# Softmax maxima taken from one group's projected queries, and four output projections in one step

## The chip, the cores and the metric

The kernel runs on one core of a Trainium2 chip. The metric is the device time of one execution in microseconds (us). A core has a matrix engine (TensorE, PE in the tables; its weight loads are PEld), a vector engine (VectorE, DVE), a scalar engine (ScalarE, ACT), a general engine (GpSimd, POOL) and a queue engine (SyncE, SP), which in this kernel issues every DMA. Each works through its own list of instructions in order and waits on semaphores where it needs a result of another.

## What is computed

Two layers, each made of attention and a feed-forward block, over 2048 positions of 448 numbers. The same weights serve both layers.

```python
def _A_ref(x, wq, wk, wv, wo):                    # x: 1 x 2048 x 448, 16 heads of 28
    q = (x @ wq).reshape(B, S, H, Dh)             # 16 heads of queries
    k = x @ wk                                    # one head of keys for all
    v = x @ wv                                    # one head of values for all
    scores = einsum(q, k) * Dh ** -0.5
    p = softmax(scores)
    return (p @ v, heads joined) @ wo
def _B_ref(x, w_gate, w_up, w_down):
    return (silu(x @ w_gate) * (x @ w_up)) @ w_down
x = x + _A_ref(layernorm(x)); x = x + _B_ref(layernorm(x))    # and both once more
```

## The kernel before, in words

Every matrix product is done with numbers split in two, a rounded high part and the rest, and two or three products are added up. The 2048 positions are cut in four chunks of 512 (`c`); the 16 heads are four groups of four (`g`). A unit of attention is one group of one chunk: 16 units, in the order of the list `GR`.

**Projection stage** (`project`, `q`, `finish`). The columns of `wq`, `wv` and `wk` lie side by side in one weight tile of 512 columns, taken in four blocks of 128 (`m`). Blocks 0 to 2 and the first 64 columns of block 3 are queries, 28 columns of block 3 are values, 28 are keys. For each chunk the blocks are taken in the order `TURN = (3, 0, 1, 2)`, 11 products each (L277). ScalarE copies a block out of PSUM, VectorE or GpSimd makes the low part (L464 to L468), and the pair goes to DRAM as `qd` (L470). After block 3, four DMAs put the keys on four places of `keys` (L476), VectorE turns the values (L478) and four DMAs put them in `vsb` (L480). The tile pair that a block is written to (`halves`) has three buffers, so a copy waits until the DMAs that read the block three before are done. A block of 128 columns holds parts of two groups, so a group's queries come together only when they are read back from DRAM by `stack` (four DMAs, L352) into one of three tiles `qstack`.

**Maxima.** The softmax needs a bound for each query. One product (L368) multiplies a tile `qstack` with a block-diagonal tile of keys (`kdiag`); `rows` (L376 to L386) turns the result on VectorE straight from PSUM, takes the largest of each 32, and one DMA (`qstack<-down`) writes the negated bound into a row of `qstack`. Three of the 16 are done in the projection stage, one of each later 13 in an attention step.

**Attention stage** (`scores`). A unit has 16 steps (`kt`), one for 128 keys: 12 score products (`step`, L541) into a tile of three PSUM banks (two such tiles take turns) and bank 7, two exponentials on ScalarE (L547 for bank 7, L548 for the three), and 4 products with the values two steps later (`pv`, L575). `between_steps` puts other work between a step's scores and the value products, at step 10 of a unit: one maxima product into the free three-bank tile; in units 9 to 12 four transposes for the next feed-forward (`flip`, L248) into the same tile; one output projection of 128 positions (12 products, `outproj`, L527) into bank 7, and its sum on VectorE (L531). A chunk's four output projections fall into four units; those of the third chunk into step 10 and step 13 of units 12 and 13.

**Feed-forward** follows, 14 blocks of the hidden width in pairs. In the first layer its last pair overlaps the first four projections of the second layer (`hand_over`). A last piece of the program, which repeats all in another form if a value ran out of range, is not executed here.

## Time and profile before

| | |
|---|---|
| three runs | 2071.49, 2077.33, 2077.23 us, median 2077.23 |
| profiled execution, its own time | 2076.66 us |
| its span, first to last instruction | 2074.9 us |
| projection of layer 1, from the first `qd` store to the first exponential | 20.0 to 78.5 us |
| attention of layer 1 | 78.5 to 614.2 us |
| feed-forward of layer 1, then projection of layer 2 | 614.2 to 1102.9 us |
| attention of layer 2 | 1102.9 to 1638.6 us |
| feed-forward of layer 2 | 1638.6 to 2074.9 us |

In the tables a row gives the busy time of a group of instructions, the mean length of one, and the time that its engine stood idle just before them, with what ended the idle time behind an arrow. "SPq" is an issue of a DMA on SyncE: the time that the issuing takes, not that of the transfer. In the chain of waits a piece "DMA" is the time from an issue to the landing of its data.

### The profile page before, as it was taken

How to read it: one execution, taken by the hardware profiler on the slowest of the kernel's cores; microseconds unless marked ns; L12 is line 12 of the kernel's file. 1: busy time of each engine (PE TensorE's matmuls, PEld its weight loads, DVE VectorE, ACT ScalarE, POOL GpSimd, SP SyncE). 2: the span in 40 equal slices, each digit the busy share in tenths (PEclk: the TensorE clock that was granted, in tenths of full speed). 3: DMA queues.
4: the chain of work that ended last, by engine and by line, in shares of the span. 5: the costliest groups of instructions: out<-in, count | busy, mean ns of one | idle time of the engine just before them, and what ended most of it. 6: DMA issues, size and time to landing. Idle time of an engine off the chain costs nothing.

```text
span 2074.9 us, 43753 instructions
## 1 busy us (share of the span) xinstructions
PE 2024.9 (98%) x18577; PEld 1303.5 (63%) x18577; DVE 507.9 (24%) x1038; ACT 1301.0 (63%) x2126; POOL 492.2 (24%) x504
## 2 busy tenths in 40 slices
PE   6999999999999999999999999999999999999998
PEld 4533333333348999999874333333333589999997
DVE  6201112112114233222460111121121152333322
ACT  2599988988883333333337998989888643333332
POOL 5202101012202333323341111111122123333321
PEclk9999999999999999999999999999999999999999
DMA  6301101011100111000132110101120001111102
GB/s 187 114 21 41 30 17 30 16 45 31 36 7 23 30 30 30 24 23 25 37 108 78 38 36 19 31 16 30 31 48 19 12 19 30 30 30 30 30 2 74
DMA packets 86590, 78.23 MB, mean 38 GB/s; under 512 B 26736, under 2 KB 66032, under 8 KB 86384
## 3 DMA queue, kind: packets, MB, share of 16 engines
q1 hardware_dynamic: 86384, 75.33, 13.2%
q8 instruction: 148, 2.42, 0.5%
q14 instruction: 58, 0.48, 0.1%
HBM read 51.51 MB, written 18.61 MB: 34 GB/s over the span
## 4 chain that ended last, share of the span: by engine, by line
PE 48%; ACT 44%; DVE 3%; issue 2%; SPq 2%; DMA 1%; POOL 0%; ACTq 0%; DVEq 0%
PE bank L299 38%; ACT pt L548 29%; ACT pt L547 14%; PE bank L527 3%; PE bank L277 3%; PE three L541 1%; PE bank L575 1%; PE bank L248 1%; PE bank L541 1%; SPq L131 1%; PE three L527 1%; DVE xl L258 0%; DVE xn L230 0%; DVE stats L217 0%; PE three L368 0%
## 5 line engine op out<-in xcount | busy, mean ns | idle before, releaser
L548 ACT ACTIVATE pt<-three 128x1536 f32<-128x1536 f32 x512 | 741.7, 1449 | 0.0
L575 PE MATMUL bank<-pt,vsb 128*32 128x512 f32 x4096 | 547.1, 607 | 0.6 <-ACT pt L548 0.6
L541 PEld LDWEIGHTS three<-qstack,keys 32*128 32x128 f32 x4608 | 253.4, 184 | 455.9 <-ACT pt L547 394.4
L541 PE MATMUL three<-qstack,keys 32*128 32x512 f32 x4608 | 503.0, 428 | 7.7 <-ACT q L467 4.4
L541 PE MATMUL bank<-qstack,keys 32*128 32x512 f32 x1536 | 494.7, 427 | 0.5 <-DVE xres L531 0.3
L299 PE MATMUL bank<-xh,wgh 64*128 64x512 f32 x1728 | 470.9, 390 | 0.5
L299 PE MATMUL bank<-xh,wgl 64*128 64x512 f32 x1404 | 382.3, 388 | 0.0
L547 ACT ACTIVATE pt<-bank 128x512 f32<-128x512 f32 x512 | 306.0, 598 | 98.6 <-PE bank L541 96.2
L299 PE MATMUL bank<-xl,wgh 64*128 64x512 f32 x1296 | 350.1, 387 | 0.0
L299 PE MATMUL bank<-wdh,h 64*128 64x448 f32 x1792 | 339.5, 362 | 1.3 <-ACT h L784 0.9
L299 PEld LDWEIGHTS bank<-xh,wgh 64*128 64x128 f32 x1728 | 287.2, 184 | 8.9 <-DVE xl L258 1.6
L299 PEld LDWEIGHTS bank<-wdh,h 64*128 64x128 f32 x1792 | 263.0, 184 | 7.7 <-issue 2.7
L609 POOL TENSOR_TENSOR o<-o 128x512 f32<-128x512 f32 x32 | 41.1, 1284 | 895.3 <-DMA o<-rd 703.3
L541 PEld LDWEIGHTS bank<-qstack,keys 32*128 32x128 f32 x1536 | 244.8, 184 | 4.9 <-DVE xres L531 3.0
L702 POOL TENSOR_TENSOR xres<-stage,xres 128x448 f32<-128x448 f32 x112 | 131.2, 1192 | 488.3 <-ACT stage L701 488.3
L299 PEld LDWEIGHTS bank<-xh,wgl 64*128 64x128 f32 x1404 | 235.3, 184 | 4.1
L306 ACT COPY seen<-bank 128x1 f32<-128x1 f32 x664 | 83.4, 164 | 235.9 <-PE bank L299 234.4
L299 PE MATMUL bank<-wdl,h 64*128 64x448 f32 x896 | 228.0, 364 | 0.0
L299 PEld LDWEIGHTS bank<-xl,wgh 64*128 64x128 f32 x1296 | 215.4, 185 | 2.8
L782 ACT ACTIVATE sg<-bank 128x512 f32<-128x512 f32 x112 | 67.0, 599 | 221.6 <-PE bank L299 212.2
L575 PEld LDWEIGHTS bank<-pt,vsb 128*32 128x32 f32 x4096 | 80.9, 108 | 189.4 <-issue 174.6
L783 DVE TENSOR_TENSOR sg<-bank,sg 128x512 f32<-128x512 f32 x112 | 77.4, 691 | 495.6 <-ACT sg L782 486.6
(115 smaller groups left out, 1731.7 us busy)
## 6 DMA issues: line engine op xcount, KB each, us to landing
qstack<-qd SPq DMA_DIRECT2D x128, 112.0 KB
qd<-q SPq DMA_DIRECT2D x24, 512.0 KB
o<-rd SPq DMA_DIRECT2D x32, 256.0 KB
wdr<-in_B_w_down_dram SPq DMA_DIRECT2D x28, 224.0 KB
wr<-in_B_w_gate_dram SPq DMA_DIRECT2D x28, 192.0 KB
wr<-in_B_w_up_dram SPq DMA_DIRECT2D x28, 192.0 KB
keys<-q SPq DMA_DIRECT2D x32, 112.0 KB
out_dram<-xres SPq DMA_DIRECT2D x16, 224.0 KB
```

The source lines that it names most:

```text
L277: nc.tensor.matmul(po, a, b, start=(i == 0), stop=(i == len(seq) - 1))
L299: nc.tensor.matmul(po, a, b, start=start, stop=stop, skip_group_check=True)
L306: nc.scalar.copy(seen[:, i : i + 1], po[:, 0:1])
L527: nc.tensor.matmul(po[:, 0:D], a[:, g, ts_], b[:, g, :], start=(g + z == 0), stop=(g == NG - 1 and z == 2))
L541: nc.tensor.matmul(three[:, j, :] if j < 3 else one, k[js, ks], q[js, part, :], start=(z == 0), stop=(z == 2), tile_position=(32 * j, 0),)
L547: nc.scalar.activation(pt1, one, AF.Exp, scale=SCALE)
L548: nc.scalar.activation(pt, three, AF.Exp, scale=SCALE)
L575: nc.tensor.matmul(accs[i][32 * j : 32 * j + 32, :], vsb[:, kt, :], pts[n][j], start=(kt == 0), stop=(kt == NT - 1), skip_group_check=True,)
L609: nc.gpsimd.tensor_tensor(rb, oraw, rb, ALU.mult)
L702: nc.gpsimd.tensor_tensor(r, s, r, ALU.add)
L782: nc.scalar.activation(sg, pg[0], AF.Silu)
L783: nc.vector.tensor_tensor(sg, pg[1], sg, ALU.mult)
```

## The change

The weight tile is laid out anew: each of the four blocks now holds the 112 queries of exactly one group, and 16 more columns. Blocks 0 and 1 carry the values in two parts (16 and 12), blocks 2 and 3 the keys in two parts; the order is `TURN = (3, 2, 0, 1)`. So a maxima product takes its moving operand straight from the block's tile, without the way through DRAM, and `kdiag` holds the keys packed in 112 rows.

- All 16 maxima products are made in the projection stage (`maxima`), three blocks after their own. For the first three units `rows` follows as before; for the other 13 the product is copied out of PSUM into a `stage` tile and written to DRAM (`kept`). In attention it is read back into an SBUF tile four steps into a unit, and `rows` works on that, four steps later.
- Each block issues one store of `qd` of 112 rows and then either four DMAs of 12 or 16 rows for `keys` or four for `vsb`; in the first chunk eight more DMAs fill `kdiag` (before: four copies on GpSimd).
- All low parts of the queries are made on VectorE; for chunks 2 and 3 of layer 1 the normalisation moves from VectorE to GpSimd.
- In layer 2 the first three blocks, made while the feed-forward still runs, are read back from DRAM (`fetch`) for their maxima products.
- A chunk's four output projections stand in one step (step 10 of units 4, 8 and 12): three into the banks of the free tile, the fourth into bank 7, and in units 8 and 12 two transposed blocks between them, in bank 7 too.

```diff
-TURN = (3, 0, 1, 2)
+TURN = (3, 2, 0, 1)
...
+            nc.gpsimd.memset(r[:, :, 252:256], 0.0)
+            rows3(r[:, :, 0:224], wq[:, 224 * z : 224 * z + 224])
+            rows3(r[:, :, 224:252], wk if z else wv)
...
+        def maxima(self, i, cands=ALL, copy=nc.scalar.copy):
+            j, moving = self.raw.pop(0)
+            assert i == j
+            pm = bank(cands)[1]
+            nc.tensor.matmul(pm, kd[0:112].rearrange("p j k -> p (j k)"), moving, start=True, stop=True)
+            if i < 3:
+                self.rows(i, pm, pers.tile([P, 512], F32, name="sg"))
+                return
+            st = self.pool.tile([P, 512], F32, name="stage", bufs=2)
+            copy(st, pm)
+            self.kept[i] = dram.tile([P, 512], F32, name=f"pm{self.layer}_{i}")
+            nc.sync.dma_start(self.kept[i], st)
...
+            while len(self.raw) > 2 and not self.far:
+                if self.raw[0][1] is None:
+                    break
+                self.maxima(self.raw[0][0])
...
-            if m == 3 or c == 0 and m == 0:
-                nc.scalar.copy(qh, po)
-                nc.vector.tensor_tensor(ql, po, qh, ALU.subtract)
-            else:
-                nc.scalar.copy(ql.bitcast(F32), po)
-                split(qh, ql, ql.bitcast(F32))
+            nc.scalar.copy(qh, po)
+            nc.vector.tensor_tensor(ql, po, qh, ALU.subtract)
...
+            d0, n = 16 * (m % 2), 12 if m % 2 else 16
+            if m > 1:
+                if c == 0 and not full:
+                    for j in range(4):
+                        dma(kd[DH * j + d0 : DH * j + d0 + n, j, :], qh[112 : 112 + n, 0:32])
+                for j in range(4):
+                    dma(keys[32 * j + d0 : 32 * j + d0 + n, :, cs], two[112 : 112 + n, :, :])
+                return
+            vt = pers.tile([P, 512], F32, name="sg")[96:128, :]
+            nc.vector.transpose(vt, po[96:128, :])
...
+            for b in range(7 - len(self.raw), 7):
+                self.maxima(self.raw[0][0], (b,), nc.vector.tensor_copy)
...
+                    c = todo.pop()
+                    ks = list({8: (0, 1), 12: (2, 3)}.get(i, ()))
+                    adds = []
+                    for t in (1, 2, 3):
+                        if ks:
+                            flip(got, X0, [ks.pop(0)], one)
+                        adds.append(outproj(c, t, free[:, t - 1, :]))
+                    for f in adds:
+                        f()
+                    outproj(c, 0, one)()
...
+                        if not full:
+                            turned = halves("m2").bitcast(F32)
+                            nc.sync.dma_start(turned[:, 0, :], self.kept.pop(i + 2))
+                    if kt == 8 and 2 < i + 2 < len(GR) and not full:
+                        self.rows(i + 2, turned[:, 0, :], turned[:, 1, :])
```

More of the change, by code (lines that the diff above doesn't have):

```diff
@@ L240, in norm, with flip @@
         return got
-    def flip(got, tiles, ks=range(4), place=None, behind=None):
+    def flip(got, tiles, ks=range(4), place=None):
         for k in ks:
@@ L248, in flip @@
                 nc.tensor.transpose(pt[:, P * t : P * t + P], got["x"][:, t, P * k : P * k + P], ident)
-            if behind is None:
-                flipped(tiles, k, pt, nc.vector.tensor_copy if place is not None else nc.scalar.copy)
-            else:
-                behind.append(lambda k=k, pt=pt: flipped(tiles, k, pt, nc.vector.tensor_copy))
+            flipped(tiles, k, pt, nc.vector.tensor_copy if place is not None else nc.scalar.copy)
     def flipped(tiles, k, pt, copy):
@@ L319, in __init__ @@
             self.steps, self.places = [], []
-            self.lent, self.plan, self.waiting, self.behind = None, {}, [], []
-            for i in range(len(GR)):
-                fs, place = (self.max_steps if full else self.quick_steps)(i)
-                if full and i == 1:
+            self.lent, self.plan, self.waiting = None, {}, []
+            self.raw, self.kept, self.far = [], {}, False
+            for i in range(len(GR) if full else 0):
+                fs, place = self.max_steps(i)
+                if i == 1:
                     fs[KC] = lambda f=fs[KC]: (f(), self.places[0]())
```

142 lines of the change are left out of this document (65 added, 77 removed).

## The prediction

> **What bounds the kernel now.** I read the page first, then the stages by window, then the interrupted steps of attention, then the chain of waits at the end of both projection stages.
>
> ```profile
> span 2074.9 us, 43753 instructions
> PE 2024.9 (98%) x18577; PEld 1303.5 (63%) x18577; DVE 507.9 (24%) x1038; ACT 1301.0 (63%) x2126; POOL 492.2 (24%) x504
> L548 ACT ACTIVATE pt<-three 128x1536 f32<-128x1536 f32 x512 | 741.7, 1449 | 0.0
> L547 ACT ACTIVATE pt<-bank 128x512 f32<-128x512 f32 x512 | 306.0, 598 | 98.6 <-PE bank L541 96.2
> ```
>
> ```profile
> 20.00:78.45 58.45, 49.90 (x228) 38.58 (x226) 33.29 (x74) 15.25 (x28) 27.27 (x43) 0.94 0.56 167
> 78.45:614.20 535.75, 529.84 (x5273) 199.61 (x5270) 75.72 (x220) 486.36 (x512) 78.96 (x79) 0.99 0.12 29
> 1049.70:1102.94 53.24, 46.99 (x259) 37.03 (x255) 25.30 (x52) 16.77 (x38) 25.55 (x34) 1.00 0.51 150
> 1102.94:1638.60 535.66, 530.11 (x5273) 199.77 (x5270) 76.32 (x220) 486.40 (x512) 78.99 (x79) 0.99 0.12 29
> ```
>
> A window row gives its length, then PE, PEld, DVE, ACT and POOL busy, the granted clock, the DMA engines' share and GB/s. The two attentions are 536 us each, and ScalarE works 486 of them: attention is bound by its exponentials. ScalarE stands idle before L547 for 98.6 us in the run, 49.3 a layer, and 96.2 of that is put down to the score products. That is what the interruptions cost, and all that the change can win there. Nothing else is won in attention, since the exponentials stay.
>
> ```profile
> 162.69 0.60 ACT L547 ACTIVATE pt<-bank 128x512 f32<-128x512 f32 x1 [0.64 <-PE bank L541]
> ...
> 254.85 1.45 ACT L548 ACTIVATE pt<-three 128x1536 f32<-128x1536 f32 x1
> ...
> 256.74 1.45 ACT L548 ACTIVATE pt<-three 128x1536 f32<-128x1536 f32 x1
> 261.55 0.60 ACT L547 ACTIVATE pt<-bank 128x512 f32<-128x512 f32 x1 [3.36 <-PE bank L541]
> ...
> 398.34 0.60 ACT L547 ACTIVATE pt<-bank 128x512 f32<-128x512 f32 x1 [4.43 <-PE bank L541]
> ...
> 511.94 0.60 ACT L547 ACTIVATE pt<-bank 128x512 f32<-128x512 f32 x1 [2.86 <-PE bank L541]
> ```
>
> A plain step lasts 1.89 us (254.85 to 256.74). A step with a maxima product alone adds 0.64 us, with an output projection 3.36, with a transposed block as well 4.43, and an output projection alone, in a free bank, 2.86. A layer has 3, 5 + 1, 4 and 2 of these: 1.9 + 20.2 + 17.7 + 5.7 = 45.5 us of its 49.3.
>
> **Attention after the change.** The step's products, on TensorE:
>
> ```profile
> 256.35 0.50 PE L368 MATMUL three<-qstack,kdiag 128*128 128x512 f32 x1 [0.21 <-ACT pt L548]
> 256.89 0.47 PE L527 MATMUL bank<-woh,onh 128*128 128x448 f32 x1
> ...
> 259.23 0.37 PE L527 MATMUL bank<-woh,onl 128*128 128x448 f32 x1
> ```
>
> Twelve products start 0.213 us apart (2.34 over 11). Alone they cost 2.86, so 0.3 us is the step's own price. Four in one step cost 48 x 0.213 + 0.3 = 10.5 us, three chunks 31.5. Joining saves only the 0.3 each, because TensorE has no slack in a plain step either: the 2.86 is almost the products' own time. Each transposed block costs 4.43 - 3.36 = 1.07; four of them 4.3. They now stand first in bank 7, which the exponential L547 frees 0.5 us later than the free tile: twice, 1.0. Sum 36.8 a layer against 45.5, a gain of 8.7. If a transposed block, whose reading by VectorE now lies under the next 36 products, costs only half, it is 10.8. I take 10 a layer, **20 us in all**. What the maxima leave behind in a unit (a read of 256 KB, six VectorE operations, one DMA) lies on VectorE, busy 76 of 536 us, and on SyncE, with more than a unit (16 x 1.89 = 30 us) until it is needed: nothing, and if late, a unit would start late.
>
> **The projection stages.** Here the instructions that are added are cheap on every engine but one. TensorE has 13 products more a layer, at most 0.5 us each (L368). ScalarE copies 10 of them (0.6 us each) and VectorE three; ScalarE is busy 15 of 58 us. VectorE takes over the low parts, 11 a layer, and one more value transpose a chunk, some 10 us onto 33 of 58. GpSimd loses 11 splits and gains, in layer 1, eight normalisations. All that has room. The queue of SyncE has not:
>
> ```profile
> L470 SPq DMA_DIRECT2D qd<-q x32: 359/422/1218, 20.0 to 1104.6; - x32
> ...
> L131 SPq DMA_DIRECT2D keys<-q x32: 807/816/1006, 20.8 to 1099.3; - x32
> L131 SPq DMA_DIRECT2D qstack<-down x32: 537/604/892, 51.5 to 1599.0; - x32
> L131 SPq DMA_DIRECT2D xd<-xh x2: 537/542/547, 638.6 to 1662.9; - x2
> ...
> L480 SPq DMA_DIRECT2D vsb<-sg x32: 586/631/1289, 24.5 to 1102.2; - x32
> ...
> L352 SPq DMA_DIRECT2D qstack<-qd x128: 322/383/1945, 30.2 to 1552.0; - x128
> ...
> L591 SPq DMA_DIRECT2D rs<-o x128: 519/586/1690, 114.3 to 1642.4; - x128
> ```
>
> These are issue times (shortest, median, longest, ns); SyncE can do nothing else meanwhile. Before, a layer's projection issues 16 stores, 16 `keys`, 16 `vsb`, 12 `qstack` and 3 `down`: 63. After: 16, 32, 32, 12 and 3, 8 for `kdiag` and 13 stores of maxima: 116 (3 more reads in layer 2). That this queue already sets the end is seen in the chain of waits of layer 2:
>
> ```profile
> 1083.83 0.71 DVE sg L478
> ...
> 1084.60 0.88 SPq L131
> ...
> 1088.16 0.66 SPq L480
> ...
> 1091.60 2.94 DMA qd<-q
> 1094.64 0.60 ACT q L464
> ...
> 1095.98 0.63 SPq L470
> ...
> 1099.32 2.55 DMA keys<-q
> 1101.97 0.59 ACT q L467
> ...
> 1106.88 1.85 PE bank L575 x5
> ```
>
> The block's store is queued behind four `keys` and four `vsb` issues, the copy of a later block waits for its buffer until that store has landed, and the first value products start at 1106.88. (In layer 1 they start at 82.10.) More issues go straight into this chain.
>
> ```profile
> 1030.68 1.84 DMA vsb<-sg
> ```
>
> ```profile
> 20.02 0.68 SPq L470 DMA_DIRECT2D qd<-q  x1
> ...
> 51.47 7.27 SPq L131 DMA_DIRECT2D qstack<-down  x3
> ```
>
> ```profile
> 82.10 1.87 PE bank L575 x8
> ```
>
> ```profile
> 1056.97 0.59 ACT L467 COPY q<-bank 128x512 f32<-128x512 f32 x1 [2.00 <-PE bank L277]
> ```
>
> The new forms (12 or 16 rows inside SBUF, stores of 112 rows) aren't in the trace. A `keys` copy of few rows is bounded by 0.54 (`xd`) and 0.82 (`keys`); I take 0.60, near the small copies inside SBUF (0.59 to 0.63). A store of 112 rows lies between 0.36 (shortest of 128 rows) and 0.68 (the first row, 64 rows); I take 0.63, as it is not a full tile either. `kdiag` 0.55, `vsb` 0.60, maxima stores 0.36 (a full tile), and 0.05 between issues.
>
> Layer 1, up to the last-but-one block's values: 15 stores 10.2, 32 `keys` 20.8, 28 `vsb` 18.2, 8 `kdiag` 4.8, `qstack` 5.7 (0.475 each with gaps), `down` 1.95, 9 maxima stores 3.7: **65 us** of issuing, from 20.0 on. To this come stalls of the queue: the three `down` wait for VectorE as they do now (7.27 in place of 1.95: 5.3), and in each of three chunks the second values' transpose waits until the first values' four DMAs have left the shared tile, about 1 us beyond the other issues; together 8.4. End at 93.8. Then, one after the other: landing 1.25 (1.84 less its own issue), transpose 0.71, four issues 2.6, a maxima store 0.41, its landing 2.4 (2.94 less 0.54), the last copy of a maximum out of bank 6, 0.7: 8.1, so that the value products begin at 101.9 in place of 82.1: **+20 us**. The last three maxima wait behind the values' DMAs because there are two `stage` tiles and one queue, and bank 6 is the accumulator.
>
> Layer 2: three blocks are out early, so the queue fills from about 1058.6 (fourth block copied at 1057 as now). From there 12 stores 8.2, 24 `keys` 15.6, 24 `vsb` 15.6, 8 `qstack` 3.8, 3 reads 1.3, `down` 1.95, 9 maxima stores 3.7: 50.1. Stalls: as above 8.4, and twice TensorE and then VectorE wait for a block read back, about 1.5 us each: 11.5. End 1120.2, and 8.1 more: 1128.3 against 1106.9, **+21.4**. A gain of 1.4 stands against it: in the last feed-forward pair a gate function waits today for `vsb` (the row at 1030.68, 1.84, of which I take most), and then the values come later, under other work.
>
> **Sum** against the profiled 2076.66: -20 + 20 + 21.4 - 1.4 = +20, so 2096.7. The profiled run is 0.6 us below the median, 2077.23. I say 2096.
>
> **Bounds.** Cheapest issues (`keys` 0.54, stores 0.4): 5.5 us less a layer, +9. If besides the stalls all lie under other issues, 8.4 and 11.5 less, -11. Dearest `keys` (0.82): 6 us more a layer, +32.
>
> **Rivals.**
>
> The queue doesn't bind: faster. If few rows make an issue as short as `qstack`'s 0.38, the 32 `keys` and 32 `vsb` lose about 0.22 each, 14 us a layer, and with stalls hidden nothing of the loss is left; the time is 2076.7 - 20 = 2057. For it: row counts do fall to a half. Against it: `rs<-o` moves 2 KB and takes 0.59 all the same, and the chain already runs through SyncE. It decides below a loss of 10 us a layer. A rule of the Trainium skill speaks for this side (DMA: Bandwidth & Descriptors, Anatomy of one DMA): there the issuing sequencer needs about 50 ns a DMA, on the software path, descriptor generation is "small, variable", and nearly all of the fixed cost is completion. As an estimate from that page, 53 more issues would be 2.7 us a layer, and the result would be near 2062. The trace's 0.38 to 0.82 us an issue disagrees, so the sum goes by the rows.
>
> The clock drops in the slowed stage: slower still.
>
> ```profile
> 53.17 0.63 PE L277 MATMUL bank<-xh,wh 128*128 128x512 f32 x1
> 53.59 0.63 PE L277 MATMUL bank<-xh,wl 128*128 128x512 f32 x1
> ```
>
> At 53 us, after a wait, products start 0.42 us apart, a block's 11 in 4.6 us; the stage's clock is 0.94. By the sum a block takes 3.8 us of the queue. If waits keep the clock low for eight blocks, each exceeds the queue by about 1.2 us with its maxima product: 10 a layer, 2117. Against it: the waits are about 1 us a block, shorter than those before 53 us. The Trainium skill (TensorE: Matmul & The Clock Gate, Part 1) has the clock halved after an idle window of some 3.4 us, which the rows here show only as halves that follow waits.
>
> **How the numbers follow.** The queue paces and the kernel is 2083 to 2110: 0.66. The clock case, above 2110: 0.06. Queue partly hidden, within 0.3% (6.2 us, about what a measurement here can tell from none): 0.08. Queue hidden, faster by more: 0.20. Slower by more than 0.3% is 0.72. The likeliest time is 2096; the range 2066 to 2110 leaves out about half of the faster case and the clock case, 0.16; if it is slower, 2083 to 2110.
>
> **What would show it.** ScalarE's idle time before its bank-7 exponential falls from 98.6 to about 79 us; three steps a layer with 10 to 13 us of idle time; no other above 1. The first value products of a layer come 15 to 25 us later against the stage's start, SyncE is issuing nearly without a gap, and the copies of a block wait for DMAs. New issues of `keys` above 0.5 us and stores of 112 rows above 0.5 show the prices; if both are near 0.4, the first rival holds. A granted clock below 0.8 in the stage speaks for the second. Wrong I'd be if the last maxima's copies were not on the way to the first value products.

## The result, and the profile after

The changed kernel takes 2135.21 us (median of 4 runs, 2134.77 to 2138.62); the kernel before took 2076.06 in the same comparison. The ratio is 1.0293 (95% interval 1.0273 to 1.0312). The forecast was 2096, range 2066 to 2110: the sign is right, the size is not, and the time lies outside the range.

The page of the changed kernel (length, the two groups of exponentials):

```profile
span 2133.2 us, 43918 instructions
L559 ACT ACTIVATE pt<-three 128x1536 f32<-128x1536 f32 x512 | 741.6, 1448 | 0.0
L558 ACT ACTIVATE pt<-bank 128x512 f32<-128x512 f32 x512 | 305.9, 597 | 115.0 <-PE bank L552 83.1
```

Its windows (for each layer the projection stage up to the first three-bank exponential, in layer 2 from the end of the feed-forward on, and then attention; length, busy PE, PEld, DVE, ACT and POOL, granted clock, DMA share, GB/s):

```profile
20.00:112.36 92.36, 56.47 (x235) 41.83 (x233) 41.30 (x82) 20.82 (x38) 21.85 (x27) 0.79 0.56 158
112.36:639.27 526.91, 520.98 (x5257) 198.64 (x5257) 76.31 (x220) 485.42 (x512) 77.65 (x77) 0.99 0.14 33
1083.70:1168.26 84.56, 48.84 (x206) 36.30 (x206) 33.20 (x64) 19.12 (x37) 5.46 (x10) 0.81 0.52 150
1168.26:1696.93 528.67, 523.05 (x5257) 200.07 (x5257) 76.47 (x220) 485.16 (x512) 77.63 (x77) 0.99 0.14 33
```

Attention is shorter by 8.8 us in layer 1 (535.75 to 526.91) and by 7.0 in layer 2. Layer 1's attention begins 33.9 us later (78.45 to 112.36). Between the end of layer 1's attention and the start of layer 2's lie 528.99 us in place of 488.73, 40.3 more. The sum, 33.9 + 40.3 - 15.8 = 58.4, is the difference of the two spans (2133.2 - 2074.9 = 58.3). So the loss is all in the two projection stages, 74 us where 41 were forecast (20 and 21.4; less the 1.4 that the forecast took off again, 40).

ScalarE's idle time before its bank-7 exponential rose to 115.0 us, though its part put down to the score products fell from 96.2 to 83.1: nearly all the rest is two waits of 14.6 and 15.4 us ahead of a layer's first exponential, at the end of the projection stages.

**The queue of SyncE**, issue times (shortest, median, longest, ns):

```profile
L131 SPq DMA_DIRECT2D keys<-q x64: 585/778/1460, 23.0 to 1152.1; - x64
L131 SPq DMA_DIRECT2D kdiag<-q x16: 582/714/868, 19.7 to 1059.1; - x16
L472 SPq DMA_DIRECT2D qd<-q x32: 309/376/530, 19.3 to 1157.8; - x32
L486 SPq DMA_DIRECT2D vsb<-sg x64: 585/599/1537, 33.0 to 1161.8; - x64
L366 SPq DMA_DIRECT2D pm<-stage x26: 319/527/632, 38.0 to 1165.7; - x26
```

From 19.3 to 101.9 us, where the value copies of the last-but-one block end, 107 DMAs are issued in 66.9 us. Between them lie 6.3 us of gaps shorter than 0.25 us each, and 9.4 us of longer stalls.

**The hole in layer 1.** ScalarE's copies of the 7th and the 8th block out of PSUM, in the kernel before and then in the changed one:

```profile
42.55 0.59 ACT L467 COPY q<-bank 128x512 f32<-128x512 f32 x1 [1.91 <-PE bank L277]
...
48.06 0.59 ACT L467 COPY q<-bank 128x512 f32<-128x512 f32 x1 [2.97 <-PE bank L277]
```

```profile
44.54 0.58 ACT L468 CAST q<-bank 128x512 fp32r<-128x512 f32 x1 [2.11 <-PE bank L359]
...
65.34 0.59 ACT L468 CAST q<-bank 128x512 fp32r<-128x512 f32 x1
```

5.5 us between the two became 20.8. Rows of the changed kernel's VectorE, then TensorE:

```profile
43.44 0.72 DVE L371 STREAM_TRANSPOSE sg<-bank 128x512 f32<-128x512 f32 x1 [4.79 <-DMA vsb<-sg]
...
54.82 0.18 DVE L380 CAST down<-flat 128x32 fp32r<-128x32 f32 x1 [3.62 <-DMA qstack<-down]
54.93 0.69 DVE L469 TENSOR_TENSOR q<-bank,q 128x512 fp32r<-128x512 f32 x1
55.65 0.72 DVE L484 STREAM_TRANSPOSE sg<-bank 32x512 f32<-32x512 f32 x1
```

```profile
56.43 1.12 PE L246 MATMUL bank<-ident,xn 128*128 128x128 f32 x4 [6.52 <-DVE sg L484]
60.20 0.80 PE L272 MATMUL bank<-xh,wh 128*128 128x512 f32 x1 [2.66 <-DVE xl L253]
```

The rows (transpose, maximum, halves) of the first three groups run on VectorE between the blocks' low parts. The first waits 4.79 us for the tile `sg`, which the value copies still hold; the third waits 3.62 us for the one tile `down`. Behind them stand the low parts, the value transpose, 3.0 us of statistics for the layernorm (56.40 to 59.42) and the second half of the transposed chunk, and TensorE waits for these. For GpSimd, to which some normalisations moved, TensorE waits nowhere in this stage.

**The end of the stage.** The chain of waits of the changed kernel in layer 1:

```profile
101.29 1.80 DMA vsb<-sg
...
103.27 0.73 DVE sg L484
...
106.64 2.21 DMA pm<-stage
...
108.97 0.70 DVE stage L364
...
109.69 2.00 DMA pm<-stage
...
111.87 0.61 ACT pt L558
...
116.49 1.85 PE bank L589 x5
```

The last block's value transpose waits for the tile that the other values hold. Then come its four copies, the stores of maxima, one more copy of a maximum and its store. Only when that has landed does the first exponential run.

**Layer 2** has two waits more, on TensorE, for blocks that are read back from DRAM:

```profile
1093.20 1.20 PE L359 MATMUL bank<-wrq,kdiag 112*128 112x512 f32 x2 [5.26 <-DMA wrq<-qd]
1106.32 0.77 PE L359 MATMUL bank<-wrq,kdiag 112*128 112x512 f32 x1 [7.34 <-DMA wrq<-qd]
```

**The joint steps** of layer 1 cost 10.5, 11.9 and 16.7 us beyond a plain one, those of layer 2 10.4, 12.2 and 17.5. In the third of layer 1, from VectorE and from TensorE:

```profile
521.84 0.71 DVE L371 STREAM_TRANSPOSE m<-m 128x512 f32<-128x512 f32 x1 [11.33 <-DMA m<-pm]
```

```profile
527.00 0.66 PE L246 MATMUL bank<-ident,xn 128*128 128x128 f32 x4 [3.25 <-DVE xl L253]
...
528.27 0.58 PE L536 MATMUL three<-woh,onh 128*128 128x448 f32 x1
528.64 0.58 PE L536 MATMUL three<-wol,onh 128*128 128x448 f32 x1
```

The last two rows are from a run of ten products, 527.90 to 531.26, that start 0.37 us apart in place of 0.21. The maxima of unit 14, read from memory, came to VectorE at 521.84, when the joint step had begun (520.44); the rows and the statistics then stood ahead of the transposed block's copies, TensorE waited 3.25 us, and soon after the wait it went on at about half its pace for those ten products (a granted clock of 0.50 from 527.9 to 531.3). The wait and 10 x 0.16 us make 4.9 us.

### The profile page after: what moved, and what is told of

Its sections match the earlier page's. It is cut to its first block, busy times and chain, and to the rows that moved or that the text cites. A ratio compares the mean times of both kernels' runs of the same rounds, so it can differ in the third digit from the quotient of the medians.

```text
span 2133.2 us, 43918 instructions
## 1 busy us (share of the span) xinstructions
PE 2027.5 (95%) x18577; PEld 1312.4 (62%) x18577; DVE 529.1 (25%) x1068; ACT 1307.4 (61%) x2148; POOL 466.3 (22%) x466
## 4 chain that ended last, share of the span: by engine, by line
PE 60%; ACT 28%; SPq 3%; DVE 2%; DMA 2%; issue 1%; POOL 0%; ACTq 0%; DVEq 0%
PE bank L294 36%; ACT pt L559 18%; PE bank L589 9%; ACT pt L558 9%; PE three L552 8%; PE bank L272 3%; PE three L536 2%; PE bank L536 2%; SPq L131 1%; SPq L486 1%; DMA m<-pm 1%; PE bank L246 1%; DMA pm<-stage 0%; PE bank L552 0%; DMA vsb<-sg 0%
## 5 line engine op out<-in xcount | busy, mean ns | idle before, releaser
L552 PE MATMUL bank<-qstack,keys 32*128 32x512 f32 x1536 | 496.4, 428 | 13.5 <-ACT pt L558 13.5
L294 PE MATMUL bank<-xh,wgh 64*128 64x512 f32 x1728 | 443.8, 391 | 0.5
L558 ACT ACTIVATE pt<-bank 128x512 f32<-128x512 f32 x512 | 305.9, 597 | 115.0 <-PE bank L552 83.1
L294 PE MATMUL bank<-xh,wgl 64*128 64x512 f32 x1404 | 365.0, 388 | 0.0
L294 PE MATMUL bank<-wdh,h 64*128 64x448 f32 x1792 | 332.5, 362 | 1.6 <-ACT h L811 1.1
L294 PE MATMUL bank<-xl,wgh 64*128 64x512 f32 x1296 | 329.7, 387 | 0.0
L294 PEld LDWEIGHTS bank<-xh,wgh 64*128 64x128 f32 x1728 | 260.4, 184 | 9.2 <-DVE xl L253 1.6
L294 PEld LDWEIGHTS bank<-wdh,h 64*128 64x128 f32 x1792 | 243.2, 185 | 8.6 <-issue 2.3
L294 PEld LDWEIGHTS bank<-xh,wgl 64*128 64x128 f32 x1404 | 215.3, 184 | 4.6
L294 PE MATMUL bank<-wdl,h 64*128 64x448 f32 x896 | 214.5, 364 | 0.0
L809 ACT ACTIVATE sg<-bank 128x512 f32<-128x512 f32 x112 | 67.1, 599 | 219.2 <-PE bank L294 210.0
L294 PEld LDWEIGHTS bank<-xl,wgh 64*128 64x128 f32 x1296 | 195.3, 185 | 3.2
```

The lines of the kernel that those rows point to most:

```text
L294: nc.tensor.matmul(po, a, b, start=start, stop=stop, skip_group_check=True)
L552: nc.tensor.matmul(three[:, j, :] if j < 3 else one, k[js, ks], q[js, part, :], start=(z == 0), stop=(z == 2), tile_position=(32 * j, 0),)
L558: nc.scalar.activation(pt1, one, AF.Exp, scale=SCALE)
L809: nc.scalar.activation(sg, pg[0], AF.Silu)
```

## The experiments

All ratios are to the kernel before. Times of stages are from each kernel's profiled run, one for each: "start" is layer 1's first three-bank exponential, "between" lies from the end of attention 1 to the first such exponential of layer 2. The letters of the theories are those of each expectation.

| kernel | us | ratio, 95% | start | attention 1 | between | attention 2 |
|---|---|---|---|---|---|---|
| before | 2076.06 | 1 | 78.45 | 535.75 | 488.73 | 535.64 |
| changed | 2135.21 | 1.0273-1.0312 | 112.36 | 526.90 | 528.99 | 528.67 |
| keys_halved | 2098.95 | 1.0094-1.0128 | 84.39 | 536.95 | 501.78 | 535.91 |
| values_halved | 2091.06 | 1.0058-1.0091 | 81.04 | 535.45 | 498.07 | 535.91 |
| joined_only | 2068.09 | 0.9950-0.9976 | 76.19 | 531.56 | 490.71 | 531.06 |
| values_by_scalar | 2153.92 | 1.0363-1.0398 | 121.45 | 522.99 | 541.57 | 522.14 |
| values_by_gpsimd | 2127.10 | 1.0224-1.0258 | 109.17 | 526.40 | 520.72 | 526.65 |
| maxima_by_scalar | 2130.42 | 1.0237-1.0270 | 116.25 | 523.90 | 530.64 | 523.25 |
| four_stages | 2131.86 | 1.0242-1.0285 | 112.08 | 525.93 | 528.26 | 526.44 |
| joined_values_gpsimd | 2061.65 | 0.9914-0.9942 | 74.22 | 528.99 | 485.00 | 530.44 |
| rows_own_tiles | 2126.56 | 1.0225-1.0260 | 106.18 | 527.08 | 527.60 | 529.49 |
| maxima_before_block | 2133.81 | 1.0268-1.0302 | 112.70 | 524.80 | 531.79 | 523.82 |
| early_read | 2130.31 | 1.0246-1.0280 | 112.91 | 527.82 | 528.37 | 523.35 |
| mended | 2124.22 | 1.0227-1.0261 | 103.29 | 524.20 | 528.85 | 526.15 |
| tail_by_scalar | 2134.12 | 1.0268-1.0303 | 115.31 | 526.31 | 528.85 | 523.55 |
| maxima_read_early | 2126.05 | 1.0225-1.0260 | 113.09 | 521.90 | 530.70 | 522.34 |
| early_maxima | 2126.71 | 1.0225-1.0269 | 114.65 | 526.33 | 523.38 | 522.18 |
| mended_all | 2118.66 | 1.0188-1.0222 | 109.99 | 521.30 | 528.82 | 521.81 |
| tail_three | 2131.43 | 1.0243-1.0278 | 112.43 | 526.98 | 526.60 | 524.75 |
| mended_three | 2107.60 | 1.0129-1.0163 | 106.17 | 521.75 | 519.75 | 521.63 |

Three things move these times without an edit, so small differences of single stages say little. Kernels with the same layer 1 stage started attention 2 us apart: 112.36 to 114.65 (changed, early_read, maxima_read_early, early_maxima), and 78.45 and 76.19 (before, joined_only). The third joint step cost 12.4 to 17.5 us in kernels whose edit does not touch it, which is up to 5 us a layer. And the last feed-forward computes for 430.0 us in every kernel, but its last results landed 6.3 to 6.7 us after that in most, 8.1 to 9.0 in four and 12.0 in values_by_gpsimd.

**Is it the number of issues?** The kernel before, with nothing but the halving of a copy:

```diff
-                dma(keys[32 * j : 32 * j + DH, :, cs], two[96 : 96 + DH, :, :])
+                dma(keys[32 * j : 32 * j + 16, :, cs], two[96:112, :, :])
+                dma(keys[32 * j + 16 : 32 * j + DH, :, cs], two[112 : 96 + DH, :, :])
```

> The kernel before, with each of the key copies issued as two, of 16 and of 12 rows: 16 issues more in layer 1's projection stage and 16 in layer 2's, the same rows and bytes. Theory A (SyncE's queue is the pace, a DMA costs by its issue): a copy of few rows was issued in 0.78 us in the changed kernel, against 0.82 for 28 rows, so each pair costs 0.8 us more; 13 us of issuing a layer, of which a part fills gaps of the queue: 8 to 13 a layer, 2093 to 2102 in all. Theory B (rows or bytes set the pace, or what is issued is hidden): 2076 within 6.

The same for the values:

```diff
-                    vsb[32 * u : 32 * u + 32, 4 * c : 4 * c + 4, 0:DH],
+                for d0, n in ((0, 16), (16, 12)):
...
+                        vsb[32 * u : 32 * u + 32, 4 * c : 4 * c + 4, d0 : d0 + n],
```

> The kernel before, with each of the value copies issued as two, of 16 and of 12 columns: 16 issues more a layer; the pieces of 112 bytes become twice as many, of 64 and 48. Theory A (issue): 16 x 0.65 = 10 us more a layer, partly in gaps: 6 to 10 a layer, 2088 to 2097. Theory B (the small pieces load the DMA engines): more than the halved keys cost, above 2102. Theory C (hidden): 2076 within 6.

Measured 23 and 15 us more: theory A both times. The halved values cost less than the halved keys, so it isn't the small pieces. In layer 1 the halvings cost 5.9 and 2.6 us (the second hardly beyond the spread), in layer 2 13.1 and 9.3; 2 us of each total are the late landing of the last results. Together the stages' parts are 31 of the 74 us that the changed kernel loses in its stages, from 32 of the 53 issues that it adds to a layer.

**What is the gain in attention?** The kernel before with the joint steps alone; the maxima products stay in attention, in step 8. As in the changed kernel, statistics for the next layernorm move from unit 8 to unit 5:

```diff
-                    if full or kt == 10 and i > 1:
+                    if full or kt == 8 and i > 1:
                         self.advance(KC if full else 1)
...
-                    if todo and kt == 10:
-                        todo.pop(0)(one)
-                    elif todo and kt == 13 and i > 11:
-                        todo.pop(0)(free[:, 0, :])
+                    if not todo or kt != 10:
+                        return
+                    c = todo.pop()
...
+                    for t in (1, 2, 3):
+                        if ks:
+                            flip(got, X0, [ks.pop(0)], one)
+                        adds.append(outproj(c, t, free[:, t - 1, :]))
```

> The kernel before, with the attention's half of the change alone: four output projections and two transposed blocks share one step, and the maxima products stay in attention, two steps earlier. In the changed kernel the three joint steps of a layer cost 10.5, 11.9 and 16.7 us, 39 together, as much as twelve single projections (12 x 2.86 = 34.3) and four blocks (4.3). Theory A: the joining gains nothing and the gain in attention (8.9 and 7.0 us a layer) is that of the maxima products, 13 x 0.64 = 8.3: 2076 within 5. Theory B, by the prediction's terms: joining gains 0.4 to 2.5 a layer: 2071 to 2076. Theory C: joining makes the gain: 2060.

It took 2068.09, 8 us less than the kernel before and between theories B and C: attention gained 4.2 and 4.6 us in the two layers. Its joint steps cost 10.2, 11.75 and 11.75, 33.7 together, where single projections and blocks cost 38.6 (12 x 2.86 and 4 x 1.07). A maxima product in a step of its own costs 0.70, 9.1 for 13. So joining is worth more than forecast. The changed kernel, which has both gains, should have had about 13.5 a layer (4.4 + 9.1) and had 8.8 and 7.0. The third joint step, 16.7 and 17.5 in place of 11.75, is most of what is missing.

**Another queue for the value copies.** First by ScalarE, later by GpSimd:

```diff
-                nc.sync.dma_start(
+                nc.scalar.dma_start(
                     vsb[32 * u : 32 * u + 32, 4 * c : 4 * c + 4, d0 : d0 + n],
```

> The changed kernel, with the value copies of the projection stages issued by ScalarE in place of SyncE: the same DMAs, 32 fewer in SyncE's queue a layer. Theory A (SyncE's issuing is the pace): 32 x 0.69 = 22 us less in the queue a layer, and then another engine paces; 12 to 20 us less a layer, 2095 to 2111. Theory B (the DMA engines, the bytes or the landing times are the pace, whoever issues): 2135 within 6. Theory C (ScalarE's copies now wait behind the copies it issues): slower than 2135.

Slower, 2153.92 (theory C). ScalarE's view of this kernel:

```profile
55.97 2.75 ACTq L486 DMA_DIRECT2D vsb<-sg  x4
58.76 1.56 ACT L252 CAST xh<-bank 128x512 fp32r<-128x512 f32 x3 [11.94 <-DMA vsb<-sg]
```

The copies of a transposed chunk stand behind the issue, which itself waits. So this run says nothing on SyncE's pace.

> The changed kernel, with the value copies of the projection stages issued by GpSimd in place of SyncE, 32 a layer. ScalarE, tried before, stood in front of its own work while it waited for the transposes and for the shared tile; GpSimd is busy a quarter of the stage and little there waits for it. Theory A (SyncE's issuing is the pace): 22 us less in SyncE's queue a layer, 2095 to 2115. Theory B (landing times or the DMA engines are the pace, whoever issues): 2135 within 6. Theory C (GpSimd issues more slowly, or its normalisations come late): above 2141.

2127.10, 8 us less: theory A's sign, but outside its range (to 2115), and outside B's (from 2129) too. In the profiled run stages and attention gained 14 us, and the late landing of the last results took 5.7 back. SyncE's issuing in layer 1 fell from 71.4 to 50.9 us, and the stage by only 3.2, since its stalls grew from 12.4 to 33.1. The largest, on SyncE's queue:

```profile
57.30 0.43 SPq L472 DMA_DIRECT2D qd<-q  x1
66.54 0.35 SPq L366 DMA_DIRECT2D pm<-stage  x1
```

That is the hole of layer 1 again: it looks as if right behind the queue stood a second chain of nearly the same length. Own tiles (below) together with this edit would show it and were not tried. In layer 2 the same edit gained 8.3.

```diff
-            nc.sync.dma_start(self.kept[i], st)
+            nc.scalar.dma_start(self.kept[i], st)
```

> The changed kernel, with the 13 stores of maxima a layer issued by ScalarE, which has made most of the copies itself. Theory A (SyncE's issuing is the pace): 13 x 0.52 = 6.8 us less in its queue a layer, and the last three stores no longer stand behind the value copies: 7 to 11 a layer, 2113 to 2121. Theory B (what paces is not the number of issues): 2135 within 6.

2130.42, within theory B's range: layer 1's start came 3.9 us later, and the gain was in attention, where the third joint step varies. It isn't a clean test of the issues, for a reason that mended_all shows below: SyncE now waited for the stores that ScalarE had issued, 11.5 us in layer 1's stage.

**The hole.** Own tiles for the first rows:

```diff
-                self.rows(i, pm, pers.tile([P, 512], F32, name="sg"))
+                side = pers.tile(..., name="sg") if self.layer else self.pool.tile(..., name="side", bufs=1)
+                self.rows(i, pm, side)
...
-            down = pers.tile([P, 32], F32R, name="down")
+            down = pers.tile([P, 32], F32R, name="down", bufs=3)
```

> The changed kernel; the first three groups' maxima get a tile of their own for the transpose in layer 1 (they shared one with the values), and three tiles in place of one for the result that is copied to the query stack, in both layers. In the changed kernel's layer 1 VectorE waited 4.79 us for the value copies to leave the shared tile and 3.62 us for the single result tile, and behind these waits stood the low parts of three blocks, a value transpose and the second half of a transposed chunk, while TensorE had no block for 20 us. Theory D (VectorE's queue in the first chunk, not SyncE's issuing, makes that hole): 5 to 8 us less, all of it in layer 1 (VectorE had no such waits there in layer 2): 2127 to 2130. Theory A (SyncE's issuing): 2135 within 3.

8.6 us less, 6.2 of it in layer 1's start: theory D. The 8th block is copied at 58.0 in place of 65.3. With the hole smaller, SyncE's queue is nearly gapless: 72.1 us of issues and 7.2 of small gaps in the 84.7 us from its first store, 5.5 of stalls. So, by this trace, the queue paces layer 1 as forecast once VectorE lets it.

The order of a maxima product and a block, the loop moved up in the code:

```diff
+            while len(self.raw) > 2 and not self.far:
+                ...
+                self.maxima(self.raw[0][0])
             cs = slice(512 * c, 512 * c + 512)
             held, po = bank(LOW, True)
```

> The changed kernel, with a waiting group's maxima product and its rows issued ahead of the next block's products in place of between that block's products and its copies. The same instructions; on VectorE the rows now lie ahead of the next block's low part by a block's products (2.5 us or more) and no longer between the products and the low part. Theory D: the low parts and value transposes of layer 1's first chunks come 4 to 8 us sooner: 2127 to 2131. Theory A: 2135 within 3. Theory E (the first product now waits for the diagonal keys in front of a block): slower by 1 to 4.

2133.81: no difference in the whole, but the stages are no shorter (0.3 and 2.8 us longer), and attention 2 is 4.8 shorter by its third joint step. Alone, the order isn't the cause.

**The end of the stage.**

```diff
-            st = self.pool.tile([P, 512], F32, name="stage", bufs=2)
+            st = self.pool.tile([P, 512], F32, name="stage", bufs=2 if self.layer else 4)
```

> The changed kernel, with four tiles in place of two for the copies of the maxima, in layer 1 alone (layer 2 has no room). Theory A (the prediction's tail: the last copies out of banks 6 and 7 wait for the stores of the earlier ones, which stand behind the last value copies): those copies are made before, the first exponential comes 5 to 6 us sooner and the first value products wait for the values alone: 2128 to 2131. Theory B (the last value copies are the end of the stage): 2135 within 2.

The first exponential came at 112.08, against 112.36: theory A's gain isn't there, and most of the 3 us that the time fell by lies in attention. The last copies of maxima were made in one go, as theory A has it (1.89 us from 105.12 on), but the first exponential still waited for the last of their stores. Then the last stores:

```diff
+            st = self.pool.tile([P, 512], F32, name="stage", bufs=2 if self.layer else 4)
...
+            (nc.sync if copy is nc.scalar.copy else nc.scalar).dma_start(self.kept[i], st)
```

> The changed kernel with four tiles for the copies of the maxima in layer 1 (alone: the first exponential did not come sooner, 112.08 against 112.36 us), and the last three stores of maxima of each layer issued by ScalarE, which is idle then, in place of SyncE, where they stand behind the value copies of two blocks. Theory G (the attention's buffers lie where the stage's tiles lay, so the first exponential waits for the last of these stores to land, and that is set by their place in SyncE's queue): layer 1 starts 3 to 5 us sooner, layer 2 (still two tiles) 1 to 3: 2124 to 2129. Theory H (the value copies themselves end the stage): 2131 to 2135.

The edit did other than its expectation says: the condition is never true, and all 13 stores of a layer went to ScalarE. It repeats maxima_by_scalar with four tiles; 2134.12, and it decides nothing. With the condition `len(cands) == 1`, which holds for the last three alone:

> What the run before was to do and did not (there all 13 stores of a layer had gone to ScalarE): the changed kernel with four tiles for the copies of the maxima in layer 1 and only the last three stores of each layer issued by ScalarE. Theory G (the first exponential waits for the last of these stores, set by their place in SyncE's queue): layer 1 starts 2 to 4 us sooner than with four tiles alone (112.1), layer 2 1 to 3: 2126 to 2131. Theory H (the value copies end the stage): 2131 to 2135.

Layer 1 starts at 112.43, as with four tiles alone; the time, 2131.43, is in theory H's range, 0.4 us above G's. VectorE and ScalarE of this run, each in its own view:

```profile
106.24 0.72 DVE L484 STREAM_TRANSPOSE sg<-bank 32x512 f32<-32x512 f32 x1 [7.21 <-DMA vsb<-sg]
106.99 1.89 DVE L364 COPY stage<-bank 128x512 f32<-128x512 f32 x3
```

```profile
107.72 1.52 ACTq L366 DMA_DIRECT2D pm<-stage  x3
```

The last copies of maxima stand on VectorE behind the last value transpose, and this waits 7.21 us for the values before it, whose copies stand in SyncE's queue. But the two edits did shorten what follows. From the last value transpose to the first three-bank exponential it took 9.1 us in the changed kernel (103.27 to 112.36), 7.7 with four tiles (104.37 to 112.08) and 6.2 here. The start doesn't show it because that transpose came 1.1 and 3.0 us later. Of the 3.0, 1.8 were there at the 8th block already (copied at 67.1), before any of these last stores. So the end hangs on the tile that the values share and on SyncE's queue, and on the last stores too: theory G's mechanism is seen in part, its gain isn't. A tile of their own for the last values was not tried.

**Layer 2's read-backs.**

```diff
-                self.soon.append([2, lambda: [a.project() for _ in range(2 - c)]])
+                self.soon.append([2, lambda: ([a.project() for _ in range(2 - c)], c and not full and a.fetch(a.raw[:2]))])
```

> The changed kernel, with the first two blocks of layer 2 read back from memory as soon as the third is out, in the feed-forward stage, in place of after it. TensorE waited 5.26 us for this read. Theory F (the wait is on the path: the two read-backs cost 5.3 and 7.3 us where the prediction had 1.5 each): 4 to 5 us less: 2130 to 2131. Theory A (SyncE's queue sets the end, the wait is made up): 2135 within 2.

TensorE's two waits became 2.56 and 10.26 us, and "between" is the same (528.37). The 5 us that the time fell by lie in attention 2, whose third joint step cost 12.6 in this run. So the time in theory F's range is luck; its mechanism isn't shown. Then the two products and the third read-back as well in the feed-forward:

```diff
+                if c and not full:
+                    self.soon.append([3, lambda: ([a.maxima(a.raw[0][0]) for _ in range(2)], a.fetch(a.raw[:1]))])
```

> The changed kernel, with the first two read-backs of layer 2, the two products that use them and the third read-back all done in the feed-forward stage. Reading the first two early alone moved TensorE's wait to the third (10.26 us in place of 7.34), and the stage was no shorter. Theory F (the two read-backs after the feed-forward, in a row, are 10 us of the stage's loss): both waits go, 8 to 12 us less, and the products in the feed-forward cost 1 to 2: 2124 to 2129. Theory A (SyncE's issuing sets the end of layer 2): 2135 within 4.

2126.71, 8.5 less. In the profiled run "between" fell by 5.6, half of what theory F says, and attention 2 by 6.5, again by its third joint step (12.4).

**The late maxima.**

```diff
+                    if kt == 0 and 2 < i + 2 < len(GR) and not full:
+                        turned = halves("m2").bitcast(F32)
+                        nc.sync.dma_start(turned[:, 0, :], self.kept.pop(i + 2))
                     if kt == 4 and 2 < i + 2 < len(GR):
                         self.stack(i + 2)
-                        if not full:
-                            ...
```

> The changed kernel, with a unit's maxima read back at the start of the unit before, ahead of the copies that wait for the sums' reciprocals, in place of at its fifth step behind them. In the changed kernel the read for unit 14 landed at 521.84 us, 7.3 us after its issue and 1.4 us into the joint step; the six operations on it and the statistics stood ahead of the transposed block's copies on VectorE, TensorE waited 3.25 us for these and then ran at half clock for 3.7 us: 16.7 us where the same step with the maxima in attention cost 11.8. Theory I: the third joint step costs 11.8 in both layers, 5 and 5.7 less: 2123 to 2127. Rival (the half clock comes with the step whatever the read does): 2135 within 3.

9.1 us less, and the third joint step is 11.76 in layer 1 and 11.74 in layer 2: theory I. ScalarE's idle time at that step, in this run:

```profile
534.29 0.60 ACT L558 ACTIVATE pt<-bank 128x512 f32<-128x512 f32 x1 [11.69 <-DVE xn L229]
```

**Do they add up?** Own tiles, the order of the products, the early read and four tiles:

> The changed kernel with the last three edits together and four tiles for the copies of the maxima in layer 1. By the theories D and F the gains add up as far as no other wait takes their place: 5 to 8, 4 to 5 and some us of the maxima's order: 2115 to 2125. By theory A alone: above 2130.

2124.22, at the upper end: as much as the own tiles alone within the intervals. Its start, 103.29, is 2.9 us sooner than theirs, "between" is that of the changed kernel. Own tiles, four tiles, the products in the feed-forward, the early maxima and the stores (all 13, as above) by ScalarE:

> The changed kernel with own tiles for the first rows (alone 8.6 us less), four tiles in layer 1, the last stores by ScalarE, the early reads of the maxima and layer 2's two products in the feed-forward. If the theories D, F, G and I hold and add up: 8 + 10 + 6 + 10 = 34 us less, near 2101, which is what the issues alone cost (halved copies of keys and values: 23 and 15 us, less the 16 gained in attention: 2098). If SyncE's issuing alone sets the end: above 2115.

2118.66: not 2101, and in the range that the expectation gives to SyncE's issuing alone (above 2115), but not for that reason. What SyncE waited for in this run between 50 and 64 us:

```profile
SPq L131 <- DMA pm<-stage: 8.1, 1, 8.1
```

A copy of keys on SyncE's queue (issued at 61.95) waited for a store that ScalarE had issued. The trace also has the semaphore that each DMA counts up, and the one that its issue waits for. All DMAs of SyncE and ScalarE take turns on the same eight semaphores (100, 102 to 104, 106 to 109). The copy waits for number 107 and counts up 107, and so do ScalarE's stores at 56.17 and 59.91. The copies that GpSimd issues in values_by_gpsimd have eight others (111 to 118). So stores that ScalarE issues late hold up SyncE, in this run as in maxima_by_scalar. And the three edits that gained alone, no DMA moved:

> The changed kernel with the three edits that gained alone: own tiles for the first rows (8.6 us), layer 2's two products in the feed-forward (8.5), the maxima read back early (9.1); no DMA is moved to another queue. If they are three separate losses, they add up: 26 us, 2109 (2106 to 2112). If SyncE's issuing stands behind each of them and takes a part back: 2115 to 2122.

2107.60: 27.6 less, where the single gains sum to 26.3. That the sums agree so well is in part luck. The gain of early_maxima alone was in good part the third joint step of attention 2, and that step is mended by the early read of the maxima as well; it can be had only once. Here start fell by 6.2, "between" by 9.2 (5.6 for early_maxima alone) and the attentions by 5.2 and 7.0. So the three losses lie in three places, the hole, layer 2's stage and the third joint steps, and mending one doesn't bring back another. Its two attentions, by windows:

```profile
106.17:627.92 521.75, 519.07 (x5257) 197.32 (x5257) 73.66 (x220) 485.41 (x512) 77.57 (x77) 0.99 0.14 33
...
1147.67:1669.30 521.63, 519.14 (x5257) 197.08 (x5257) 73.58 (x220) 485.05 (x512) 77.62 (x77) 0.99 0.14 33
```

Attention now gains 14.0 us a layer over the kernel before. What is left against it are stages 27.7 and 31.0 us longer than before. Of these 58.7 the halved copies account for 31, as they cost in the kernel before. How the other 28 share out among stores of maxima, `kdiag` and the end was not separated.

**A version that beats both.** The joint steps, and before's value copies, 16 a layer, by GpSimd:

```diff
-                nc.sync.dma_start(
+                nc.gpsimd.dma_start(
                     vsb[32 * u : 32 * u + 32, 4 * c : 4 * c + 4, 0:DH],
```

> The kernel with the joined output projections alone (2068), and beside it the value copies of the projection stages, 16 a layer, issued by GpSimd. Theory A (the chain at the end of a stage runs through SyncE's queue in the kernel before as well): 16 x 0.66 = 10.6 us less in the queue, of which TensorE, busy 50 of 58 us, leaves 2 to 5 a layer: 2058 to 2064. Theory B (the queue does not bind at 63 issues): 2068 within 3. Theory C (GpSimd's splits of the blocks come later for it): above 2071.

2061.65 us, ratio 0.9928 (0.9914 to 0.9942): theory A. It is 6.4 us below the joint steps alone; "between" is 5.7 shorter, and layer 1 starts 2.0 us sooner, which is no more than the spread. So SyncE's issues cost time at 63 a layer too, at least in layer 2, as the prediction read from its chain.

## Why the prediction was right and wrong

**Right: that it gets slower, where, and that SyncE's issues are a large part of it.** Halving copies and nothing else costs what the queue's theory says, 31 of the stages' 74 us. That the queue carries the rest as well isn't shown.

**Wrong: the size.** The forecast was 20 us more; the two spans differ by 58. Of the 38 us between, layer 1's stage has 14 (33.9 for 20), layer 2's stage 20 (40.3 for 21.4 - 1.4) and the attentions 4 (15.8 gained for 20). Counted to the first value products, layer 1's 14 are about 8 for the prices of the issues, 1 for stalls and 6 for the end. Layer 2's are about 5 for issues, 5 for stalls, 7 for the end, 2 for a later beginning and the 1.4 that did not come. The terms one by one:

**Wrong: the price of an issue.** Up to layer 1's last-but-one block the forecast had 65 us of issues with their gaps; they were 66.9 + 6.3 = 73.2. `keys` took 0.78 in place of 0.60, `kdiag` 0.71 for 0.55, stores of maxima 0.53 for 0.36, and the values 0.69 in the mean (22.2 us for 32 in layer 1) for 0.60; only the stores of 112 rows were cheaper, 0.38 for 0.63. With the stalls, the queue reaches that point at 101.9 in place of 93.8. The forecast's 5.3 + 3.1 us of stalls up to there were 9.4. In layer 2 the issues are 54.7 for 50.1 and the stalls 17.0 for 11.5.

**Wrong: the end, forecast at 8.1 us.** From the last-but-one block's value copies to the first value products it took 14.5 us in layer 1 and 15.2 in layer 2. The forecast had the value products wait for a copy out of bank 6 and nothing after it. In fact the first exponentials wait too, until the store of that copy has landed, 2.0 us later (at 111.87 the first one starts), and the value products follow them by 4.6 us.

**Wrong: "all that has room" for VectorE.** Its 41.3 us of 92.4 in layer 1 do fit; but what counts is the order on it. The first three groups' rows, put between the low parts, carry two waits (8.4 us) into everything behind them. Taken away, they gave 6.2 us. They hid in the forecast's stalls of the queue, which were nearly right in sum by luck, so they didn't make the error of the sum. They make a second chain about as long as the queue, which is the likely reason why taking 20 us of issues away gained 3 there.

**Wrong: two read-backs at 1.5 us each.** TensorE waited 5.3 and 7.3; moving both out of the way took 5.6 us off layer 2's stage.

**Wrong: maxima in attention leave "nothing" behind.** They left a read that lands late, and behind it the joint step: 5 us in layer 1, 5.7 in layer 2. The clause "if late, a unit would start late" looked at the unit and not at VectorE's queue, where the late operations stand ahead of a transposed block. Against it joining was worth 4.4 a layer where the forecast's terms left 0.4 to 2.5 beside the maxima, so the term of 20 us came to 15.8.

**Wrong: 1.4 us for the gate function.** It isn't to be seen: from attention 1's end to the first block's products after the feed-forward lie 445.9 us in both kernels (614.20 to 1060.09, 639.27 to 1085.15).

**The rivals.** The hidden queue is refuted by the halved copies: 32 added issues cost 23 us, 0.7 each. The Trainium skill (DMA: Bandwidth & Descriptors, Anatomy of one DMA) has about 50 ns for the dispatch, for the path of DMAs that GpSimd issues. It can't be carried over to SyncE, whose medians here are 0.38 to 0.78 us an issue, and GpSimd's own issues took 0.55 (values_by_gpsimd). The clock rival's sign appeared, 0.79 and 0.81 in the stages against 0.94 and 1.00, but mostly not as the pace: on the four blocks after the hole TensorE waited 0.7 to 0.8 us each, for ScalarE's copies of the maxima, and a block's 11 products took 2.8 us. In the hole itself the 8th block's products took 4.2 us, 1.4 of them by the low clock. The Trainium skill (TensorE: Matmul & The Clock Gate, Part 1) has the clock halved after an idle window of about 3.4 us, whose place is free; in the third joint step half pace followed a wait of 3.25 us, near that figure and a little below it.

## What to carry to other kernels

Where a queue issues DMAs back to back, count the issues and price each by the same shape of copy; here fewer bytes and rows did not pay for a second issue (0.78 us for 12 rows, 0.82 for 28). An engine that is idle half of the time is still full if an operation that waits stands ahead of those which others wait for: look for shared or single tiles between a DMA and an in-order engine. Before a DMA is given to another engine, look which semaphores it will count on and whose work will stand behind it. Work that was moved through memory came back late here, and its cost was that of what stood behind it.

## What was not expected of the hardware

The price of an issue depends on the number of rows, but doesn't fall with it. The same copy of `keys`, in SyncE's rows of the changed kernel, four of 12 rows and then four of 16:

```profile
22.96 3.34 SPq L131 DMA_DIRECT2D keys<-q  x4
...
29.69 2.58 SPq L131 DMA_DIRECT2D keys<-q  x4
```

Issues of 12 rows take 0.78 to 0.87 us, as 28 rows did before (0.81 to 0.93, one 1.01); those of 16 rows mostly 0.59 to 0.68. The values' copies of 32 rows take 0.60. So of the copies inside SBUF those of 12 and 28 rows are dear and those of 16 and 32 cheap; why isn't shown. The forecast's "near the small copies" held for 16 rows alone.

And moving a DMA from SyncE to ScalarE does not part the two queues: in this program both take turns on the same eight semaphores, so a DMA of SyncE waited 8.1 us for one issued by ScalarE (mended_all). GpSimd's have semaphores of their own. With the value copies, that was the move that gained: 2127.10 and 2061.65 against 2135.21 and 2068.09.
